# Merging a unit's last small products with the next unit's first ones, and a new order for unit 0, in a scan kernel followed by a two-layer network

## The chip, the core and the metric

The kernel runs on one core of one Trainium2 chip. The time is in microseconds (us) on the device, from launch to end. The kernel before took 334.04 us, the median of three runs (333.22 to 334.71). Engines are named as in the profile: PE (TensorE, matrix products), DVE (VectorE), ACT (ScalarE), POOL (GpSimd), SP (SyncE, which here only issues DMAs).

## What is computed

```python
# x (4, 8, 768, 32), a (4, 8, 768), B and C (4, 8, 768, 16): float32; chunk = 32
log_a = np.log(np.clip(a, 1e-06, 1.0))
for c in range(nc):                                   # chunks of the sequence
    cum = np.cumsum(la, axis=-1)
    L = np.exp(cum[:, :, :, None] - cum[:, :, None, :]) * causal
    M = np.einsum('bhin,bhjn->bhij', Cc, Bc) * L
    y_intra = np.einsum('bhij,bhjd->bhid', M, xc)
    y_inter = np.einsum('bhin,bhnd->bhid', Cc, state) * np.exp(cum)[:, :, :, None]
    y[:, :, sl] = y_intra + y_inter
    Bx = np.einsum('bhjn,bhjd->bhjnd', Bc, xc) * np.exp(cum[:, :, -1:] - cum)[:, :, :, None, None]
    state = np.exp(np.sum(la, axis=-1))[:, :, None, None] * state + np.sum(Bx, axis=2)
# y -> (3072, 256)
h = y @ w_in                                          # w_in (256, 2048)
out = (h * (1.0 / (1.0 + np.exp(-h)))) @ w_out        # w_out (2048, 256); the weights come as 64-bit floats
```

## The kernel before

**Two halves of the work.** The scan runs in units of 256 time steps: three units for each of the four batches, twelve in all, numbered 0 to 11. The network after it runs in passes of two units (512 tokens). Pass 0 is units 0 and 1, pass 1 is units 2 and 3, and so on to pass 5. While a pass of the network runs, the scan prepares the two units of the next pass.

**A unit of the scan** is made of these pieces; the letters are those of the functions and of the plan:
- loads (`L`, or `load_x`, `load_n`, `load_t`, `load_ab`, `load_pa` one by one): x, B, C and two forms of a.
- `T` (`f_T`, `f_T2`; for units 1 and 2 `f_TP` on PE): B and C are transposed, on DVE, and ACT masks the transposed C by parity of the head into `ce`.
- `P` (`f_P`, after `f_P0` clips its input): the prefix products of a, `pfx`, one scan on DVE. `C` (`f_C`): `cw` is the transposed C times `pfx`.
- `1` and `2` (`f_E1`; `f_Ab` and `f_Ek` for units 0 and 1): the decays `E` inside chunks of 64, in two scans on DVE. `B` (`f_B`): `BT`, which is B times the last decay of each chunk.
- `D`: `f_G` (line 440, the products of C and B, in tiles of 32 by 64 of the array) and `f_D0` (line 426, the products of `BT` and x, in tiles of 64 by 32), one burst on PE.
- `S`, `s` and `M`: the states between chunks (DVE), their masked copies `sm` (ACT), and the products of line 440 times `E`, written over `E` (two instructions of DVE).
- `Y`: `f_Y`, first the state products (line 480, tiles of 32 by 64), then those of the masked `E` and x (line 489, tiles of 64 by 32), one burst on PE; `f_X` copies the result to `xf` on ACT.
- `h`, `l`, `d`: `xf` is split into three parts, `xh` (ACT), `xl` and `xd` (DVE), the inputs of the network.

**PSUM.** Four of the eight banks form one tile (`bank4`) with a single buffer. The products of `D`, the result of `Y` and `B2`, a sum of the network, take it in turn. Two banks are `half` (the network's first layer, and some of the early products), two are `acc` (its output).

**A step of the network** (`step`) is a block of 128 of the 2048 hidden columns; a pass has 16 steps, f = 0 to 15. In a step PE does four products of the first layer (line 565), two of a correction for the next step (line 557), and four of the second layer for the step three earlier (lines 599 and 600); all have 512 columns. The two correction products of the second layer (line 613, `s2_d`) go into `B2`; where the four banks are in use by the scan they are put off (`PENDING`) and done together later. ACT scales (line 559), applies the activation and rounds it to `gh`. DVE makes `gl` (line 579) and `gd` (line 583); in six of the steps of passes 2 to 4 (`ASIDE`), `gl` is made by POOL. At f = 2 the outputs of the pass before are put together by DVE (lines 634 and 639), which frees `B2`.

**What sets the order.** Every engine's instructions stand in the order in which the program issues them (the schedule is manual). For passes 1 to 4 a plan says after which step each piece of the two units `a` and `b` of the next pass is issued:

```python
PLAN = {0: ("aPC",), 1: ("a1", "bL"), 3: ("aD",), 4: ("aSsM",), 5: ("aY",), 6: ("ah", "bT"), 7: ("bPC",), 8: ("b1", "aL"),
        9: ("bD",), 10: ("bSsM",), 11: ("bY",), 12: ("bh", "ald"), 13: ("bld",), 15: ("aT",)}
FIRST = {2: "a2B", 9: "b2B"}
```

`FIRST` is issued right after the large products of the first layer. The products of line 613 are put off while f is below 6 or 9 to 11. Pass 0 is written out by hand (`steps` and the text after it), since in it the weights are also brought from 64-bit to 32-bit floats: two casts on ACT (`w_size`), three instructions on DVE (`w_bits`, lines 201, 203 and 204), an addition on POOL (line 209).

**The start.** SP issues in this order: a by chunks (`ach`), C of unit 0, x of unit 0, the prefix input `pa01` of units 0 and 1 together, weights 0 to 2, then B and x of unit 1. `f_Ab` broadcasts a to the partitions by products on PE, and `f_Ek` scans from PSUM. `f_A2` (line 276) later clips a of the other batches (`acl`), which is loaded behind weight 6.

Of the kernel before, what the change touches and what calls it, by code (L numbers as in the profile page):

```python
# [33 lines left out]
def kernel(  # L34
# [49 lines left out]
    NB = 76  # L84
# [113 lines left out]
    def w_bits(n, parts=1):  # L198
        if n in raw:
            u, v, hi = two(wu.pop(n)), two(wv.pop(n)).bitcast(U32), raw[n][:, :, :, 1]  # L200
            nc.vector.tensor_scalar(out=u, in0=u, scalar1=LEAST, scalar2=MOST, op0=ALU.max, op1=ALU.min)
            u = u.bitcast(U32)
            nc.vector.tensor_scalar(out=u, in0=u, scalar1=3, scalar2=None, op0=ALU.logical_shift_left)
            nc.vector.scalar_tensor_tensor(out=v, in0=hi, scalar=0x80000000, in1=v,  # L204
                                           op0=ALU.bitwise_and, op1=ALU.bitwise_or)
            w32[n] = block("w32")
            for i in range(parts):
                fs = slice(WF // parts * i, WF // parts * (i + 1))
                nc.gpsimd.tensor_tensor(out=two(w32[n])[:, :, fs].bitcast(U32), in0=u[:, :, fs], in1=v[:, :, fs],  # L209
                                        op=ALU.add)  # L210
        if n == 3:
            load_w(n + RAW, nc.sync)
# [25 lines left out]
    pa01, pa2 = block("pa01"), block("pa2")  # L238
# [4 lines left out]
    def load_a(t, t0, n):  # L243
        nc.sync.dma_start(out=t[:, 0:n], in_=bass.AP(tensor=a.tensor, offset=a.offset + t0, ap=[[S, H], [0, N], [1, n]]))

    load_t(0, 1, nc.sync)
    load_n(0, 0, nc.scalar)
    load_x(0, nc.sync)
    load_a(pa01, 0, 2 * UT)
    for n in range(3):  # L250
        load_w(n, nc.sync)
    load_n(1, 0, nc.sync)
    load_x(1, nc.sync)

    def f_A():
        nc.vector.tensor_scalar(out=ach[A0:A1], in0=ach[A0:A1], scalar1=1.0, scalar2=1e-6, op0=ALU.min, op1=ALU.max)
        nc.vector.memset(ach[A0:A1, :, 0:1], 0.0)
        nc.sync.dma_start(out=a_first, in_=ach[A0:A1])
        load_w(3, nc.sync)
        load_w(4, nc.sync)  # L260
        load_a(pa2, 2 * UT, UT)
        load_ab(2, nc.sync)
        load_w(5, nc.sync)
        load_n(2, 1, nc.sync)
# [30 lines left out]
    def busy(n, small=0):  # L295
        t = half("zero")
        for i in range(n):
            nc.tensor.matmul(out=t, lhsT=idle[:, 0:128], rhs=idle, start=True, stop=True)
        for i in range(small):
            nc.tensor.matmul(out=t[:64, :64], lhsT=idle[:, 0:64], rhs=idle[:, 64:128], start=True, stop=True)  # L300
# [39 lines left out]
    def f_P0(u, engine):  # L340
        src = (pa2[:, 0:UT] if u == 2 else pa01[:, UT * u:UT * u + UT]).rearrange("p (c t) -> p c t", t=Q)
        PZ[u] = (pz, pz1, pz)[u]
        engine.tensor_scalar(out=PZ[u][:, :, 1:], in0=src, scalar1=1.0, scalar2=1e-6, op0=ALU.min, op1=ALU.max)
# [8 lines left out]
    def scan_E(u, g0, n, t):  # L352
        if g0 == 0:
            E[u] = sc.tile([128, 2, H, Q], FP32, name="E")
# [5 lines left out]
    def f_Ab(u, k):  # L360
        ab[u, k] = t = acc("ab").rearrange("p (h t) -> p h t", t=Q)
        n = 4 if u == 0 else H
        for h in range(0, H, n):
            nc.tensor.matmul(out=t[:, h:h + n].rearrange("p h t -> p (h t)"),  # L364
                             lhsT=sel[:A1, 2 * u + k].rearrange("r c m -> r (c m)"),
                             rhs=ach[:A1, h:h + n].rearrange("r h t -> r (h t)"), start=True, stop=True,
                             skip_group_check=True)

    def f_Ek(u, k, hs=slice(0, H)):
        t = ab[u, k] if hs.stop < H else ab.pop((u, k))  # L370
        scan_E(u, H * k + hs.start, hs.stop - hs.start, t[:, hs])
# [46 lines left out]
    def f_D0(u, ts=(0, 1, 2, 3)):  # L418
# [4 lines left out]
        for t in ts[:3 if last else 4]:  # L423
            k, c = divmod(t, 2)
            for g in range(4):
                nc.tensor.matmul(out=d[c][32 * g:32 * g + 32, k],  # L426
                                 lhsT=bt[64 * c:64 * c + 64, k, 32 * g:32 * g + 32],
                                 rhs=xc[64 * c:64 * c + 64, k, 64 * g:64 * g + 64], start=True, stop=True,
                                 tile_position=(64 * c, 32 * g), skip_group_check=True)
        BX[u] = d  # L430
        if 3 in ts:
            BT.pop(u)
# [37 lines left out]
    def f_Y(u):  # L470
        first = u % UPB == 0
        sp, cw, m, xc = SM.pop(u), CW.pop(u), E.pop(u), xt.pop(u)
        DP.pop(u)
        BX.pop(u)
        y = GY[u] = bank4()
        for t in range(1 if first else 0, 4):
            k, c = divmod(t, 2)
            for g in range(4):
# [3 lines left out]
                                 start=(k == 0 or (first and t == 2)), stop=False,  # L482
                                 tile_position=(32 * g, 64 * q), skip_group_check=True)
        for k in range(2):
            for w in range(2):
                for c in range(2):
                    for q in range(4):
# [4 lines left out]
                                         skip_group_check=True)  # L492

# [171 lines left out]
    f_P0(1, nc.gpsimd)  # L665
    load_n(1, 1, nc.gpsimd)
    f_Ab(0, 0)
    f_Ab(0, 1)
    f_TP(0)
    f_Ek(0, 0, slice(0, 4))  # L670
    f_Ek(0, 0, slice(4, 8))
    f_T(0, 1)
    for e in range(2):
        f_T2(0, e)
    f_Ek(0, 1, slice(0, 4))
    f_Ek(0, 1, slice(4, 8))
    f_B(0)
    busy(1, 10)
    f_G(0)
    f_D0(0)  # L680
    f_P(0)
    f_C(0, nc.gpsimd)
    f_A0()
    f_M(0, 0)
# [3 lines left out]
    w_size(0)  # L688
# [9 lines left out]
    w_bits(1, 2)  # L698
    f_s1(0, 0)
# [36 lines left out]
    def stage(u, what):  # L736
        for c in what:
# [6 lines left out]
            elif c == "T":  # L744
                if 0 < u < UPB:
                    f_TP(u)
                else:
                    f_T(u, 0)
                    f_T(u, 1)
                f_T2(u, 0)  # L750
# [19 lines left out]
            elif c == "Y":  # L770
                f_Y(u)
                f_X(u)
            elif c == "h":
# [9 lines left out]
    def todo(text):  # L783

        for step in text.split():
            if ":" in step:
# [6 lines left out]
    steps = ((1, 0, ""), (0, 3, "2:PTC1 s6"), (1, 1, "b5 2:2Ba"), (1, 2, "3:x b6 r11 s7"), (1, 3, ""),  # L793
             (0, 4, "2:DSsM r12"), (1, 4, "b7 r13 s8"), (0, 5, "3:T s9"), (1, 5, "2:Y b8 r14"), (0, 6, "3:1PC s10"),
             (1, 6, "b9 r15 3:2B s11 h0 l0"), (0, 7, "2:h s12"), (1, 7, "3:D b10 3:SsM"))
# [3 lines left out]
    for text in ("m0 b11 s13 2:l h1 l1", "m1 3:Y b12 s14 2:d d0 4:L 3:h h2 l2", "m2 b13 s15 3:l d1 h3 l3",  # L799
# [7 lines left out]
    PLAN = {0: ("aPC",), 1: ("a1", "bL"), 3: ("aD",), 4: ("aSsM",), 5: ("aY",), 6: ("ah", "bT"), 7: ("bPC",), 8: ("b1", "aL"),  # L807
            9: ("bD",), 10: ("bSsM",), 11: ("bY",), 12: ("bh", "ald"), 13: ("bld",), 15: ("aT",)}
    FIRST = {2: "a2B", 9: "b2B"}

    ASIDE = (2, 4, 5, 6, 10, 15)
    PENDING = []

    PARTS = {3: 10, 5: 11, 7: 12, 8: 6, 10: 13, 11: 7, 12: 14, 13: 15}

    def step(s):
# [12 lines left out]
        if scans and f in FIRST:  # L829
            stage(2 * P + 2 + "ab".index(FIRST[f][0]), FIRST[f][1:])  # L830
# [24 lines left out]
        if PENDING and not (scans and (f < 6 or 9 <= f < 12)):  # L855
            s2_d(PENDING)
            PENDING.clear()
        if scans and f == 8:
            f_sum2(P)
        if 1 <= s <= last:  # L860
            s1_gl(s - 1, nc.gpsimd if f in ASIDE and scans and P > 1 else nc.vector)
# [5 lines left out]
        if scans:  # L867
            for what in PLAN.get(f, ()):
                u = 2 * P + 2 + "ab".index(what[0])
                if f == 15 or what == "aL":  # L870
                    u += 2
                if u < NU:
                    stage(u, what[1:])
# [39 lines left out]
```

## Time and profile before

| what | value |
|---|---|
| median of three runs | 334.04 us (333.22 to 334.71) |
| the profiled execution | 334.14 us |
| its span, first to last instruction | 332.4 us, 7727 instructions |
| PE, DVE, ACT, POOL busy | 96%, 76%, 66%, 23% of the span |
| granted clock of PE | 0.996 of full speed |
| DMA | 30.80 MB, mean 93 GB/s |
| small products: lines 440, 426, 480, 489 | 8.3, 5.3, 7.9, 10.3 us busy |
| gd (line 583), gl on DVE and on POOL (line 579) | 59.6, 42.8 and 29.4 us busy |

Busy times come from one profiled execution on the chip. Products on PE are pipelined: one of 512 columns is listed with 0.39 us, but the next one starts 0.227 us after it, so costs on PE are read from the starts. The same holds on DVE, where the start of the next instruction comes a little before the listed end of the last one. `x32` behind a line of the timeline means that so many records in a row are merged into it; a small 32-bit product leaves two records, and a few records can be missing. A figure in brackets is the idle time of the engine before the instruction and what ended it.

### The profile page before, as it was taken

The numbers are of one execution on the slowest core, as the hardware profiler recorded it, in microseconds if no ns is written. First come the engines' busy times: TensorE is split into PE (matmuls) and PEld (weight loads), VectorE is DVE, ScalarE is ACT, GpSimd is POOL, SyncE is SP. The second block draws the span as 40 slices with busy tenths as digits, with TensorE's granted clock in tenths as the row PEclk, the third lists the DMA queues.
The fourth block names the chain that finished last, engine by engine and source line by source line (L and its number), as shares of the span: only waits on it lengthen the run. The fifth ranks groups of instructions, "written<-read, shape, count | busy, mean of one in ns | idle before, by whom it ended". The sixth has DMA issues, their size and how long they took to land.

```text
span 332.4 us, 7727 instructions
## 1 busy us (share of the span) xinstructions
PE 319.0 (96%) x3123; PEld 254.9 (77%) x3123; DVE 253.8 (76%) x417; ACT 218.2 (66%) x417; POOL 77.6 (23%) x77
## 2 busy tenths in 40 slices
PE   7679999999999999999999999999999999999992
PEld 4467788888878788778788778788778788888881
DVE  6794999998786987996866996866996764674453
ACT  3557488656488898667757667767657756666651
POOL 3744335465011121240202240202240202000000
PEclk9999999999999999999999999999999999999998
DMA  6999679676672863354600353600452000021003
GB/s 134 223 272 269 187 182 300 135 122 103 143 115 57 155 108 63 65 105 86 129 4 0 68 108 82 126 4 0 91 92 44 2 2 0 0 45 21 0 0 63
DMA packets 92683, 30.80 MB, mean 93 GB/s; under 512 B 77564, under 2 KB 83708, under 8 KB 92648
## 3 DMA queue, kind: packets, MB, share of 16 engines
q1 hardware_dynamic: 83848, 25.20, 34.3%
q0 software_dynamic: 2528, 4.59, 7.9%
q10 hardware_dynamic: 6272, 0.52, 1.3%
q8 instruction: 24, 0.39, 0.5%
q14 instruction: 11, 0.09, 0.1%
HBM read 22.79 MB, written 3.32 MB: 79 GB/s over the span
## 4 chain that ended last, share of the span: by engine, by line
PE 90%; DVE 3%; issue 2%; DMA 2%; SPq 1%; ACT 1%; POOL 1%; DVEq 0%; POOLq 0%; ACTq 0%
PE hp L565 23%; PE b L613 11%; PE hp L557 11%; PE oa L599 11%; PE oa L600 11%; PE oa L542 8%; PE hp L529 8%; PE gy L489 3%; PE gy L480 2%; PE gy L440 2%; DMA pa<-in_a_dram 2%; PE gy L426 1%; POOL w L209 1%; SPq L135 0%; DVE wv L204 0%
## 5 line engine op out<-in xcount | busy, mean ns | idle before, releaser
L559 ACT ACTIVATE hp<-hp 128x512 f32<-128x512 f32 x80 | 46.6, 582 | 68.1 <-PE hp L557 68.0
L579 DVE TENSOR_TENSOR gl<-g,gh 128x512 fp32r<-128x512 f32 x62 | 42.8, 690 | 50.2 <-ACT gh L575 47.2
L565 PE MATMUL hp<-xh,wh 128*128 128x512 f32 x160 | 65.3, 408 | 0.0
L583 DVE SCALAR_TENSOR_TENSOR gd<-gh,g 128x512 fp32r<-128x512 f32 x80 | 59.6, 748 | 5.1 <-ACT gh L575 5.1
L565 PE MATMUL hp<-xl,wl 128*128 128x512 f32 x160 | 62.5, 391 | 0.0
L599 PE MATMUL oa<-gh,wh 128*128 128x512 f32 x160 | 62.4, 390 | 0.0
L600 PE MATMUL oa<-gl,wl 128*128 128x512 f32 x160 | 62.3, 390 | 0.0
L579 POOL TENSOR_TENSOR gl<-g,gh 128x512 fp32r<-128x512 f32 x18 | 29.4, 1631 | 121.7 <-ACT gh L575 121.7
L575 ACT ACTIVATE gh<-g 128x512 fp32r<-128x512 f32 x80 | 50.6, 632 | 2.7
L557 PE MATMUL hp<-xd,wd 128*128 128x512 f32 x160 | 49.5, 391 | 0.0
L573 ACT ACTIVATE g<-hp 128x512 f32<-128x512 f32 x80 | 47.5, 594 | 0.5 <-PE hp L565 0.5
L613 PE MATMUL b<-gd,wd 128*128 128x512 f32 x160 | 44.3, 390 | 0.0
L565 PEld LDWEIGHTS hp<-xh,wh 128*128 128x128 f32 x160 | 30.0, 187 | 9.2 <-ACT hp L559 2.6
L557 PEld LDWEIGHTS hp<-xd,wd 128*128 128x128 f32 x160 | 30.0, 188 | 6.5
L599 PEld LDWEIGHTS oa<-gh,wh 128*128 128x128 f32 x160 | 30.0, 188 | 6.4
L613 PEld LDWEIGHTS b<-gd,wd 128*128 128x128 f32 x160 | 29.9, 188 | 6.5 <-DVE o L639 0.3
L600 PEld LDWEIGHTS oa<-gl,wl 128*128 128x128 f32 x160 | 30.0, 188 | 6.3
L565 PEld LDWEIGHTS hp<-xl,wl 128*128 128x128 f32 x160 | 30.1, 188 | 5.2
L529 PE MATMUL hp<-xf,w 128*128 128x256 f32 x128 | 29.8, 386 | 3.0 <-POOL w L209 1.7
L355 DVE TENSOR_TENSOR_SCAN E<-ab,diag 128x512 f32<-128x512 f32 (+1 forms) x26 | 29.2, 1153 | 2.0 <-PE ab L364 1.5
L209 POOL TENSOR_TENSOR w<-wu,wv 128x512 uint32<-128x512 uint32 (+1 forms) x20 | 24.1, 1212 | 27.2 <-DVE wv L204 27.1
L529 PEld LDWEIGHTS hp<-xf,w 128*128 128x128 f32 x128 | 23.7, 190 | 8.0 <-POOL w L209 2.8
(87 smaller groups left out, 384.7 us busy)
## 6 DMA issues: line engine op xcount, KB each, us to landing
ab<-a_zero SPq DMA_DIRECT2D x18, 256.0 KB
raw<-in_moe_w_in_dram SPq DMA_DIRECT2D x8, 512.0 KB
raw<-in_moe_w_out_dram SPq DMA_DIRECT2D x8, 512.0 KB
wl<-w POOLq DMA_DIRECT2D x16, 256.0 KB, 3.8
xt<-in_x_dram SPq DMA_DIRECT2D x22, 128.0 KB
out_dram<-ot SPq DMA_DIRECT2D x44, 64.0 KB
bn<-in_B_dram SPq DMA_DIRECT2D x20, 64.0 KB
tbc<-in_C_dram SPq DMA_DIRECT2D x20, 64.0 KB
```

What stands on the lines that cost most here:

```text
L355: nc.vector.tensor_tensor_scan(out=E[u].rearrange("p k h t -> p (k h t)")[:, Q * g0:Q * (g0 + n)], data0=t.rearrange("p g t -> p (g t)"), ...
L529: nc.tensor.matmul(out=hp[:, i], lhsT=two(w32[j])[:, kc, 128 * i:128 * i + 128], rhs=two(XF[u])[:, kc], start=(kc == 0), stop=(kc == KC - 1))
L557: nc.tensor.matmul(out=HP[s], lhsT=two(WD[f // 2])[:, kc, 128 * (f % 2):128 * (f % 2) + 128], rhs=XD[P][:, kc], start=(kc == 0), stop=Fals ...
L559: nc.scalar.activation(HP[s], HP[s], AF.Copy, scale=-HALF / UP)
L565: nc.tensor.matmul(out=HP[s], lhsT=two(w[f // 2])[:, kc, 128 * (f % 2):128 * (f % 2) + 128], rhs=x_[P][:, kc], start=False, stop=(kc == KC ...
L573: nc.scalar.activation(G[s], HP.pop(s), AF.Silu, scale=UP)
L575: nc.scalar.activation(GH[s], G[s], AF.Copy, scale=DOWN)
L579: engine.tensor_tensor(out=GL[s], in0=G[s], in1=GH[s].bitcast(FP32), op=ALU.subtract)
L583: nc.vector.scalar_tensor_tensor(out=GD[s], in0=GH[s].bitcast(FP32), scalar=1.0 + 1.0 / HALF, in1=G.pop(s), op0=ALU.mult, op1=ALU.subtract)
L599: nc.tensor.matmul(out=OA[P][m], lhsT=two(WH[n])[:, r, ms], rhs=gh, start=(f == 0), stop=False)
L600: nc.tensor.matmul(out=OA[P][m], lhsT=two(WL[n])[:, r, ms], rhs=gl, start=False, stop=(f == NF - 1))
L613: nc.tensor.matmul(out=B2[P][:, m], lhsT=two(WD[n])[:, r, 128 * m:128 * m + 128], rhs=gd, start=(fresh and s == tiles[0]), stop=True, skip ...
```

## The change

Three things are changed together.

**The merged burst.** `f_Y` is cut into `f_Ys` (state products) and `f_Ym` (the rest). A new function `f_YG(u)`, letter `Z`, issues for a unit and the one before it: the products of `f_G(u)`, a drain of PE, the state products of unit u - 1, `f_D0(u)`, the rest of unit u - 1's `Y`. The result of unit u - 1 goes into columns 384 to 511 of the same four banks that hold unit u's products. `E` gets a second buffer, and the pool of 2 KB blocks has 74 instead of 76.

**The plan.** Passes 1, 2 and 3 to 4 have plans of their own, in which seven pairs of units are merged (2/3, 4/5, 6/7, 7/8, 8/9, 9/10, 10/11). The pieces of the units move by up to four steps, the products of line 613 are put off to other steps (`OWN`, `LEAVE`), and POOL makes `gl` in other steps (`ASIDE`), 18 times as before. `A` and `B` are the units of the pass after next; `<` marks what is issued right after the first layer's products.

**Unit 0.** The prefix input is loaded unit by unit, unit 0's ahead of x and unit 1's behind weight 1. The broadcast products of unit 0 go to separate banks, `f_G` comes ahead of the last scan, the first `f_M` ahead of the prefix scan, and the two casts of weight 0 ahead of `f_SM`. POOL takes `cw` first, then C's load of unit 1 and the clip of unit 1; the zero columns (`f_A0`) are written later. The three instructions of `w_bits` on weight 0 are done in two halves.

```diff
-    NB = 76
+    NB = 74
...
     load_t(0, 1, nc.sync)
     load_n(0, 0, nc.scalar)
+    load_a(0)
     load_x(0, nc.sync)
-    load_a(pa01, 0, 2 * UT)
-    for n in range(3):
+    for n in range(2):
         load_w(n, nc.sync)
+    load_a(1)
+    load_w(2, nc.sync)
...
+    def f_YG(u):
+        GY[u - 1] = new_dp(u)[:, :, 384:512]
+        f_G(u)
+        nc.tensor.drain()
+        f_Ys(u - 1)
+        f_D0(u, False)
+        f_Ym(u - 1)
...
     f_P0(0, nc.gpsimd)
-    f_P0(1, nc.gpsimd)
-    load_n(1, 1, nc.gpsimd)
-    f_Ab(0, 0)
-    f_Ab(0, 1)
+    f_Ab(0, 0, slice(0, 4))
+    f_Ab(0, 0, slice(4, 8))
+    f_Ab(0, 1, slice(0, 4), half)
     f_TP(0)
     f_Ek(0, 0, slice(0, 4))
-    f_Ek(0, 0, slice(4, 8))
     f_T(0, 1)
     for e in range(2):
         f_T2(0, e)
+    f_Ab(0, 1, slice(4, 8))
+    f_Ek(0, 0, slice(4, 8))
     f_Ek(0, 1, slice(0, 4))
+    busy(1, 10, new_dp(0)[:, 0])
+    f_G(0)
     f_Ek(0, 1, slice(4, 8))
     f_B(0)
-    busy(1, 10)
-    f_G(0)
     f_D0(0)
+    f_M(0, 0)
+    w_size(0)
     f_P(0)
     f_C(0, nc.gpsimd)
-    f_A0()
-    f_M(0, 0)
+    load_n(1, 1, nc.gpsimd)
+    f_P0(1, nc.gpsimd)
     f_S(0)
     f_SM(0)
     f_M(0, 1)
-    w_size(0)
     w_bits(0, 2)
...
     w_bits(1, 2)
+    f_A0()
...
-    steps = ((1, 0, ""), (0, 3, "2:PTC1 s6"), (1, 1, "b5 2:2Ba"), (1, 2, "3:x b6 r11 s7"), (1, 3, ""),
-             (0, 4, "2:DSsM r12"), (1, 4, "b7 r13 s8"), (0, 5, "3:T s9"), (1, 5, "2:Y b8 r14"), (0, 6, "3:1PC s10"),
-             (1, 6, "b9 r15 3:2B s11 h0 l0"), (0, 7, "2:h s12"), (1, 7, "3:D b10 3:SsM"))
+    steps = ((1, 0, ""), (0, 3, "2:PTtC1 s6"), (1, 1, "b5 2:2Ba"), (1, 2, "3:x b6 r11 s7"), (1, 3, ""),
+             (0, 4, "2:DSsM r12"), (1, 4, "b7 r13 s8"), (0, 5, "3:T s9"), (1, 5, "b8 r14"), (0, 6, "3:t1P s10"),
+             (1, 6, "b9 r15 3:2B s11 h0 l0"), (0, 7, "3:Z s12"), (1, 7, "b10 3:CSsM"))
...
-    ASIDE = (2, 4, 5, 6, 10, 15)
+    PLAN1 = {0: ("atP1",), 1: ("a2B",), 2: ("aC", "bL"), 3: ("aD",), 4: ("aSsM", "bT"), 5: ("bP1",), 6: ("bt2B",),
+             7: ("bZ",), 8: ("bSM", "AL"), 9: ("bsC", "ah"), 10: ("ald",), 11: ("bY",), 12: ("bh",), 13: ("bld",),
+             15: ("AT",)}
+    PLAN2 = {0: ("atP1",), 1: ("a2B",), 2: ("aC", "bL"), 3: ("aD",), 4: ("aSM", "bT"), 5: ("as", "bP1"), 6: ("bt2B",),
+             7: ("bZ",), 8: ("bSM", "AL"), 9: ("bsC", "ah", "AT"), 10: ("ald", "AtP"), 11: ("A12",),
+             12: ("<AB", "AZ"), 13: ("bh", "ASM"), 14: ("<bld", "As", "BL"), 15: ("AC", "BT")}
+    PLAN3 = {0: ("btP1",), 1: ("b2B",), 3: ("bZ",), 4: ("bSM",), 5: ("bsC", "AL"), 6: ("ah",), 7: ("ald", "AT"),
+             8: ("AtP1",), 9: ("A2B",), 11: ("AZ",), 12: ("bh", "ASM"), 13: ("<bld", "AsC", "BL"), 15: ("BT",)}
+    OWN = {1: (9, 10, 13, 14, 15), 2: (10, 11, 15), 3: (6, 7, 8, 9, 10, 14, 15)}
+    LEAVE = {1: 10, 2: 11, 3: 10}
+    ASIDE = {1: (), 2: (4, 6, 8, 11, 13, 15), 3: (0, 4, 8, 9, 12, 15)}
```

`t` is the masking part of the old `T` (`f_T2`). With `OWN` the products of line 613 are done only in the named steps of a pass that has a scan beside it, and `LEAVE` is the step after which their sum is copied out of the banks.

## The prediction

> **What bounds the kernel now.** I read the page first: engine totals, the 40 slices, the chain that ended last.
>
> ```profile
> PE 319.0 (96%) x3123; PEld 254.9 (77%) x3123; DVE 253.8 (76%) x417; ACT 218.2 (66%) x417; POOL 77.6 (23%) x77
> PE   7679999999999999999999999999999999999992
> DVE  6794999998786987996866996866996764674453
> DMA  6999679676672863354600353600452000021003
> PE 90%; DVE 3%; issue 2%; DMA 2%; SPq 1%; ACT 1%; POOL 1%; DVEq 0%; POOLq 0%; ACTq 0%
> ```
>
> TensorE (PE) is full from the fourth slice on, and the chain is 90% PE. By stretches PE is busy in all but 0.1 us from 40 to 320 us. So every nanosecond that PE saves after 34.1 us is a gain, and every wait put into its queue there is a loss. Before 34.1 us DMA is full and VectorE (DVE) nearly so. I therefore looked at PE around two bursts of small products, in its timeline (start, us busy): a Y burst, then a G and D0 burst.
>
> ```profile
> 97.09 0.39 PE L600 MATMUL oa<-gl,wl 128*128 128x512 f32 x1
> 97.41 0.69 PE L480 MATMUL gy<-cw,sm 32*64 32x64 f32 x32
> 98.04 0.86 PE L489 MATMUL gy<-E,xt 64*32 64x64 f32 x64
> 98.83 0.50 PE L565 MATMUL hp<-xh,wh 128*128 128x512 f32 x1
> 99.16 0.39 PE L565 MATMUL hp<-xl,wl 128*128 128x512 f32 x1
> ...
> 110.53 0.39 PE L600 MATMUL oa<-gl,wl 128*128 128x512 f32 x1
> 110.85 0.69 PE L440 MATMUL gy<-ce,bh 32*64 32x128 f32 x32
> 111.47 0.43 PE L426 MATMUL gy<-xt,BT 64*32 64x64 f32 x24
> 111.83 0.50 PE L565 MATMUL hp<-xh,wh 128*128 128x512 f32 x1
> 112.17 0.40 PE L565 MATMUL hp<-xl,wl 128*128 128x512 f32 x1
> ```
>
> Large products start every 0.227 us (99.16, 99.39, 99.62 in the same timeline). Entering a burst takes 0.32 (97.09 to 97.41), 0.09 too much. Leaving it costs about 0.25: 0.15 from the last small start to the large one, and 0.11 because the next large start comes after 0.33 and not 0.227. Inside, the tile shape changes once: the last L440 start to the first L426 start is 0.198, L480 to L489 0.147, against 0.01 to 0.02 between equals.
>
> **Part 1: the merged burst.** Seven pairs are merged: units 2/3, 4/5, 6/7, 7/8, 8/9, 9/10, 10/11. A Y and a G/D0 burst carry overheads of 0.09 + 0.147 + 0.25 and 0.09 + 0.198 + 0.25, together 1.03 us. The new order is G, drain, state products, D0, rest of Y: one entry 0.09, the drain x, one shape change 0.147, one exit 0.25, so 0.49 + x. The number of products is the same. No drain of PE is in the trace. Nearest row for x: the change from L440 to L426, 0.198, where the array also empties; upper end: 0.45, that plus 0.25 for a queue that starts anew. I take 0.3, near the row. Saving 0.24 per pair, 0.1 to 0.34; for seven 1.7 us (0.6 to 2.4).
>
> A rule speaks against sharing banks. TensorEngine Tiling (Array Packing), Gotcha 1, says that different row tiles cannot access one PSUM bank simultaneously. Here L480 already sends row groups 0 and 1 to the same bank, and its 32 records start within 0.63 us, 20 ns apart, so the row shows no taking of turns. By the rule I would price the shared part at one 0.22 us product after another, some 3.5 us per pair (an estimate), and the change would lose over 20 us.
>
> **Part 2: what the merged burst waits for.** D0 needs BT, the last DVE product of the new unit (L383), and now stands in PE's queue ahead of all later large products; a late BT holds everything. Before, the second unit of a pass had six steps between D0 of the first and its own; now it has four (step 3 to step 7), shorter ones, because L613 (0.45 per step) is put off. So I walk DVE, by start-to-start times: gl and gd 0.60 each (113.41, 114.01), S 1.1, M 1.2 (94.98 to 96.18), transposes 1.03, wd 0.60, prefix scan 0.8, half an E scan 1.17 (two in 2.33), BT 0.4, two output transposes 1.22, cw 0.35.
>
> Pass 1 (units 4/5): DVE starts at 92.62 after D0 of unit 4. Three gl/gd pairs 3.66, S 1.14, M 1.2, transposes 1.03, wd 0.6, prefix 0.8, E 2.34, BT 0.4: 11.2, ready at 103.8. PE: step 4 from 92.60 to 95.01, three steps of ten large products at 0.227 to 101.82, entry 0.09, G 0.43, drain 0.3, state products 0.48, change 0.147: D0 at 103.27. Wait 0.5 (0 to 1.0).
>
> Pass 2 (units 6/7): the output sums come first and end at 141.0. The rows of DVE, and those of GpSimd (POOL) beside them:
>
> ```profile
> 139.81 1.27 DVE L639 SCALAR_TENSOR_TENSOR o<-b,o 128x512 f32<-128x512 f32 x2
> 142.21 2.38 DVE L583 SCALAR_TENSOR_TENSOR gd<-gh,g 128x512 fp32r<-128x512 f32 x2
> 148.67 1.15 DVE L583 SCALAR_TENSOR_TENSOR gd<-gh,g 128x512 fp32r<-128x512 f32 x1
> ...
> 142.07 1.36 POOL L579 TENSOR_TENSOR gl<-g,gh 128x512 fp32r<-128x512 f32 x1 [3.66 <-ACT gh L575]
> 147.99 1.29 POOL L579 TENSOR_TENSOR gl<-g,gh 128x512 fp32r<-128x512 f32 x1 [1.01 <-ACT gh L575]
> ```
>
> From 141.0: three gl/gd pairs 3.66, cw 0.35, two single gd 1.2, S 1.07, M 1.2, transposes 1.05, output transposes 1.22, prefix 0.8, E 2.34, BT 0.4: 13.3, ready at 154.3. PE: step 5 starts at 144.56, three steps to 151.37, D0 as above 1.45 later at 152.82. Wait 1.5. But two gl run on POOL in the stretch, and the rows show what that does: two gd take 2.38 instead of 1.2 beside one, one takes 1.15 instead of 0.69 beside another; a third, at 145.68, cost 0.07. Mean of 1.18, 0.46, 0.07: 0.57. Two of them add 1.15 (0.1 to 2.4). I take a wait of 2.65 (1.5 to 3.9).
>
> SBUF — State Buffer, in "SBUF: two separate sides", has the pair of ports that DVE and GpSimd share as a lock for the whole instruction. The two gd agree with it (lost 1.18 beside 1.36), the third case does not. By the rule two full gl would be lost, 1.36 + 1.29, and the wait would be 4.15 (an estimate).
>
> Units 2/3, ahead of the passes: DVE is free at 46.75 after unit 3's transposes and a weight step. One E scan 1.82 (47.35 to 49.17), prefix 0.71, weight step 1.40, E 1.25, BT 1.24 (52.87 to 54.11): 53.2. PE reaches 45.8, then three groups of eight at 0.2155, 50.9, plus 1.45: 52.4. Wait 0.8 (0 to 0.9; 0 if POOL does not slow E and BT).
>
> For 7/8, 8/9, 9/10 and 10/11 BT is ready: it ends one step or more ahead, or ahead of the output sums on which G waits already (PE idle under 0.1 at 141.14). No wait there.
>
> **Part 3: unit 0.** Its first Y burst starts at 13.81 after PE idled 2.55 on POOL's cw, which stands behind the prefix input (landed by 9.6) and two DMA issues (10.97 to 13.04). The new order takes cw ahead of these issues, puts M into DVE's idle 1.24 ahead of the prefix scan, and loads a half-sized prefix input before x. On DVE the first scan waits for one product instead of two (about 4.7, was 5.46); four scans at 0.6, a transpose 0.5, BT 0.4 end at 8.0, M (0.6, after G) at 8.9, prefix 9.6, S 10.7. On ACT sm (0.6) now stands behind weight 0's two casts (1.2), and the weight lands at about 10; so Y starts at about 11.9, 1.9 earlier (an estimate). What is late next:
>
> ```profile
> 32.46 0.42 DVE L276 TENSOR_SCALAR acl<-acl 36x512 f32<-36x512 f32 x1 [2.92 <-DMA acl<-in_a_dram]
> 33.62 0.42 DVE L410 TENSOR_TENSOR cw<-tp,pfx 128x256 f32<-128x256 f32 x1
> ...
> 34.10 5.45 PE L529 MATMUL hp<-xf,w 128*128 128x256 f32 x24 [0.54 <-DVE cw L410]
> ```
>
> DVE waits 2.92 for acl, whose DMA is queued behind the weights; DMA's share is 1.11 from 18 to 32 us. PE waits at 34.10 for unit 2's cw, which follows acl. Neither order moves acl, so PE still resumes at about 34.1 and only idles longer ahead of it. Worth 0, between -1.9 (acl lands earlier by as much) and +0.4: the zero-column DMAs of POOL (13.66 to 15.08, beside a DMA share of 0.63 to 1.01) move into the full stretch.
>
> Edits at nothing: three more DVE instructions for weight 0 and the finer first products lie ahead of the acl wait; uncovered they cost 0.3. Put-off L613 products are as many as before; their bank is free in time (M of unit 7 at about 159, the first L613 at about 162). POOL keeps 18 gl. The loads of unit 8 now land one step ahead of their transposes, but SP is not held by the steps; if they did land late, all of DVE would wait behind the transposes. The second E tile and two blocks fewer: no wait on a block is in the trace.
>
> **Sum.** -1.7 + 0.8 + 0.5 + 2.65 + 0 = +2.25. The profiled execution took 334.14 (span 332.4); that is 0.10 over the median of 334.04. 334.04 + 2.25 = 336.3 us.
>
> **The rivals.** (1) BT in time, not slower: DVE reaches BT of unit 7 before 152.8 and that of units 3 and 5 before 52.4 and 103.3. For it: DVE idles 0.95 and 1.59 between 150.8 and 155.9, so its queue is not always full. Against: those idle stretches lie behind the six steps that are now four. It gives -1.7, 332.3; it decides when the three waits sum to less than 1.7. (2) The start carries through: acl lands 1.9 earlier. For it: DMA has a gap at 16 to 17 us (share 0.63). Against: 1.11 afterwards. It gives 336.3 - 1.9 = 334.4. (3) The merge does not save what it says: x at 0.53 eats both ends. For it: no row shows a drain. With the same waits +3.95, 338.0.
>
> **How the numbers follow.** About 0.5% (1.67 us) is what a measurement of this kernel can tell from no change. The forecast 0.50, of which 0.06 lies within 0.5% (waits at their low ends: 0 + 0.2 + 1.5 - 1.7); rival 1 0.18, of which 0.03 is within 0.5%; rival 2 0.18, within; rival 3 0.14, slower. Faster 0.15, same 0.27, slower 0.58. Range: below, rival 1 at 332.3; above, all waits at their high ends (0.9 + 1.0 + 3.9) with a saving of 1.7 make 338.2, and with rival 3 a little over; I take 338.6. The forecast's own range is 335.0 to 338.2.
>
> **What would show it.** Right: PE idle of 2 to 4 us in front of D0 of unit 7 with BT as its releaser, smaller ones in front of units 3 and 5; PE's wait for unit 2's cw grown from 0.54 to some 2.4, ending at about 34; merged bursts 0.2 to 0.3 shorter than two. Wrong: no idle after 34.1, or a first continuous PE stretch that starts clearly before 33.

## The result, and the profile after

The changed kernel took 343.2 us (median of four runs, 342.46 to 344.0); the kernel before took 333.81 beside it (median of four). The ratio is 1.028 (95% interval 1.024 to 1.032). Slower was right, but the size was not: I had forecast 336.3 with a range up to 338.6. In all that follows, executions over 1.5% above the fastest of the same kernel are left out of medians and ratios. The profiled execution took 343.85 (span 342.1), 9.7 more than that of before.

The page of the changed kernel: the totals, two rows of the 40 slices, and the chain that ended last.

```profile
PE 322.9 (94%) x3122; PEld 257.2 (75%) x3123; DVE 253.3 (74%) x420; ACT 217.2 (63%) x417; POOL 77.9 (23%) x77
...
PE   8878998999999999995999999899999999999993
...
PEclk9998999999999999998999999999999999999999
...
PE 72%; DVE 14%; DMA 4%; ACT 3%; issue 3%; SPq 2%; POOL 1%; DVEq 0%; POOLq 0%; ACTq 0%
```

The chain shows most: PE carried 90% before and carries 72% now. DVE, and DMA behind it, took the difference. The PE row has a new gap in slice 19 (the wait for BT of unit 7). The clock has an 8 in slices 4 and 19; before, it was all nines until the end:

```profile
PEclk9999999999999999999999999999999999999998
```

I made a ledger by comparing the starts of the same products in both traces (first-layer products of pass 0, then each step of the passes), and of each burst with those it replaces:

| place | predicted | measured |
|---|---|---|
| unit 0 and the start, until 37 us | 0 | +0.7 |
| units 2/3 (waited 0.96 for BT) | +0.6 | +1.1 |
| pass 1, with units 4/5 (no BT wait) | +0.3 | +1.4 |
| units 6/7 (waited 3.60 for BT), and the slow products behind | +2.4 | +5.1 |
| the other four merged bursts | -1.0 | -0.6 |
| pass 3, late loads of unit 10 | 0 | +1.6 |
| rest, several small waits | 0 | +0.5 |

The first row is one draw of several. In the eleven traces that have the new unit 0 and no added products, the offset at that place lies between -1.45 and +2.47 (median -0.40).

**A merged burst without a wait**, units 7/8 in PE's timeline, answers to the two bursts of before:

```profile
178.10 0.69 PE L440 MATMUL gy<-ce,bh 32*64 32x128 f32 x32
178.95 0.69 PE L477 MATMUL gy<-cw,sm 32*64 32x64 f32 x32 [0.15 <-issue]
179.57 0.43 PE L427 MATMUL gy<-xt,BT 64*32 64x64 f32 x24
179.82 0.86 PE L491 MATMUL gy<-E,xt 64*32 64x64 f32 x64
180.61 0.50 PE L582 MATMUL hp<-xh,wh 128*128 128x512 f32 x1
```

The drain shows as 0.15 of "issue" idle. From the last start of line 440 to the first of line 477 it is 0.42 in six of the seven bursts (0.55 in that of units 4/5); I had taken 0.3. The step from line 477 to 427 costs 0.147, as predicted. The records still start some 20 ns apart although two units share the banks, so the price taken from the row held, and the one worked out from the rule on banks did not.

**The wait for BT**, PE's timeline at unit 7, and behind it two windows (length, busy time of PE, PEld, DVE, ACT, POOL, granted clock, DMA share, GB/s):

```profile
155.75 0.58 PE L477 MATMUL gy<-cw,sm 32*64 32x64 f32 x24 [0.15 <-issue]
159.93 0.58 PE L427 MATMUL gy<-xt,BT 64*32 64x64 f32 x32 [3.60 <-DVE BT L384]
```

```profile
160.00:163.50 3.50, 3.50 (x101) 2.94 (x102) 2.83 (x8) 0.66 (x2) 0.00 (x0) 0.52 0.34 85
163.50:167.00 3.50, 3.50 (x16) 2.61 (x15) 2.28 (x4) 2.34 (x5) 0.00 (x0) 0.99 0.56 86
```

The predicted wait is there, larger. What I had no term for is the clock: for 3.41 us after the wait PE runs at half of it, and large products start every 0.427 instead of 0.227. From the last large product ahead of the burst to the twentieth behind it PE takes 12.52. In gl_off (below), where the wait is 1.39 shorter and no half clock follows, it takes 9.76. So the clock costs 1.4 more.

**Why BT was late**, DVE's timeline in pass 2, three instructions that take 0.60 alone, from start to start:

```profile
145.80 1.79 DVE L596 TENSOR_TENSOR gl<-g,gh 128x512 fp32r<-128x512 f32 x1
...
152.00 1.17 DVE L596 TENSOR_TENSOR gl<-g,gh 128x512 fp32r<-128x512 f32 x1
...
156.60 1.68 DVE L600 SCALAR_TENSOR_TENSOR gd<-gh,g 128x512 fp32r<-128x512 f32 x1
```

POOL makes gl at 145.51 (1.53), 151.31 (1.31) and 156.13 (1.60). By start-to-start times DVE loses 1.11, 0.49 and 1.01, in all 2.6. DVE runs two steps behind PE here, so a third gl fell ahead of BT; I had counted two.

**The start**, PE's timeline in unit 1's Y burst:

```profile
24.52 0.43 PE L491 MATMUL gy<-E,xt 64*32 64x64 f32 x27
25.95 0.63 PE L491 MATMUL gy<-E,xt 64*32 64x64 f32 x37 [1.00 <-issue]
27.05 5.37 PE L546 MATMUL hp<-xf,w 128*128 128x256 f32 x16 [0.47 <-ACT xf L516]
```

Unit 0's Y starts at 12.25 (predicted 11.9), and PE is 1.30 ahead until 24 us. Then it waits 1.00 for nothing that the profile names, and from 27.0 to 30.4 the clock is half: the lead of 1.30 has become a lag of 1.55. (Of the wait for unit 2's cw, 0.54 before, nothing is left, since PE is late by more.)

**Pass 3**, timeline of all engines, shows a chain of four:

```profile
217.09 0.68 DVE L389 STREAM_TRANSPOSE bh<-tbc 128x256 f32<-128x256 f32 x1 [3.61 <-DMA tbc<-in_B_dram]
...
219.87 0.91 ACT L407 ACTIVATE ce<-ct,par 128x256 f32<-128x256 f32 x2 [2.14 <-DVE ct L389]
...
221.31 0.50 PE L582 MATMUL hp<-xh,wh 128*128 128x512 f32 x1 [1.35 <-ACT hp L576]
```

SP issues eight output stores from 208.34 (4.13 long), and the loads of unit 10 behind them from 212.51. DVE waits in its queue for the loads, ACT's mask waits for DVE, ACT's scaling waits behind the mask, and PE waits for that.

### The profile page after: what moved, and what is told of

Its sections match the earlier page's. It is cut to its first block, busy times and chain, and to the rows that moved or that the text cites. A ratio compares the mean times of both kernels' runs of the same rounds, so it can differ in the third digit from the quotient of the medians.

```text
span 342.1 us, 7749 instructions
## 1 busy us (share of the span) xinstructions
PE 322.9 (94%) x3122; PEld 257.2 (75%) x3123; DVE 253.3 (74%) x420; ACT 217.2 (63%) x417; POOL 77.9 (23%) x77
## 4 chain that ended last, share of the span: by engine, by line
PE 72%; DVE 14%; DMA 4%; ACT 3%; issue 3%; SPq 2%; POOL 1%; DVEq 0%; POOLq 0%; ACTq 0%
PE hp L582 19%; PE b L630 9%; PE hp L574 9%; PE oa L559 8%; PE oa L616 8%; PE oa L617 8%; PE hp L546 5%; PE gy L491 2%; DVE gd L600 2%; DVE gl L596 2%; DVE E L360 2%; DMA raw<-in_moe_w_in_dram 2%; PE gy L477 1%; DMA wl<-w 1%; DMA tbc<-in_C_dram 1%
## 5 line engine op out<-in xcount | busy, mean ns | idle before, releaser
L596 DVE TENSOR_TENSOR gl<-g,gh 128x512 fp32r<-128x512 f32 x62 | 45.1, 728 | 36.5 <-ACT gh L592 34.8
L582 PE MATMUL hp<-xh,wh 128*128 128x512 f32 x160 | 66.1, 413 | 1.6 <-ACT hp L576 1.6
L600 DVE SCALAR_TENSOR_TENSOR gd<-gh,g 128x512 fp32r<-128x512 f32 x80 | 60.5, 764 | 9.0 <-ACT gh L592 6.8
L582 PE MATMUL hp<-xl,wl 128*128 128x512 f32 x160 | 63.2, 395 | 0.1
L630 PE MATMUL b<-gd,wd 128*128 128x512 f32 x160 | 43.4, 390 | 0.0
L582 PEld LDWEIGHTS hp<-xl,wl 128*128 128x128 f32 x160 | 30.4, 190 | 5.5 <-DMA wl<-w 0.6
L546 PE MATMUL hp<-xf,w 128*128 128x256 f32 x128 | 31.1, 400 | 2.6 <-POOL w L212 1.7
L212 POOL TENSOR_TENSOR w<-wu,wv 128x512 uint32<-128x512 uint32 (+1 forms) x20 | 25.2, 1268 | 27.2 <-DVE wv L210 27.1
L546 PEld LDWEIGHTS hp<-xf,w 128*128 128x128 f32 x128 | 24.9, 199 | 7.8 <-POOL w L212 3.1
```

What stands on the lines that cost most here:

```text
L546: nc.tensor.matmul(out=hp[:, i], lhsT=two(w32[j])[:, kc, 128 * i:128 * i + 128], rhs=two(XF[u])[:, kc], start=(kc == 0), stop=(kc == KC - 1))
L582: nc.tensor.matmul(out=HP[s], lhsT=two(w[f // 2])[:, kc, 128 * (f % 2):128 * (f % 2) + 128], rhs=x_[P][:, kc], start=False, stop=(kc == KC ...
L596: engine.tensor_tensor(out=GL[s], in0=G[s], in1=GH[s].bitcast(FP32), op=ALU.subtract)
L600: nc.vector.scalar_tensor_tensor(out=GD[s], in0=GH[s].bitcast(FP32), scalar=1.0 + 1.0 / HALF, in1=G.pop(s), op0=ALU.mult, op1=ALU.subtract)
L630: nc.tensor.matmul(out=B2[P][:, m], lhsT=two(WD[n])[:, r, 128 * m:128 * m + 128], rhs=gd, start=(fresh and s == tiles[0]), stop=True, skip ...
```

## The experiments

The kernel before took 333.8 to 335.8 beside the different runs, so each ratio is against the runs beside it. Beside fill67, al_early, old_start and new_start it took 335.75, with a granted clock down to 0.981. These four ratios therefore come out low, by some 0.5% (new_start has 0.994 there and 0.999 in its second measurement), and the readings rest on the traces. Offsets are those of a step's first product against the trace of before.

**The clock behind the wait (fill67).**

```diff
         GY[u - 1] = new_dp(u)[:, :, 384:512]
+        if u == 7:
+            busy(12, 0, new_dp(u)[:, 0])
         f_G(u)
```

> The changed kernel with 12 products on constants (0.227 each, 2.7 us) in front of the merged burst of units 6 and 7, inside its wait of 3.6. Theory A, that a wait of over 3.4 costs twice, because PE then runs 3.41 us at half clock: the wait shrinks to about 0.9, D0 still starts at BT's end, no half clock after it, so 1.4 to 1.7 less than the changed kernel, about 341.7. Theory B, that the slow products after the wait come from the queue or the operands and not from the idle time: no change, 343.2, half clock as before. If the products delay anything on the path themselves: slower than 343.2.

341.81 us, ratio 1.018 (1.013 to 1.023).

```profile
159.08 0.46 PE L427 MATMUL gy<-xt,BT 64*32 64x64 f32 x32 [0.95 <-DVE BT L384]
```

The wait is 0.95, and the trace has no half clock before the end of the work. The stretch of 12.52 is 11.31 here: twelve useless products inside the wait made it 1.2 shorter, so the slow products come with the idle time. All six traces in which unit 7 waits 3.55 to 3.60 (changed kernel, al_early, own12, p01_old, old_start, after_shift) have a half clock there.

**POOL beside DVE (gl_off).**

```diff
-    ASIDE = {1: (), 2: (4, 6, 8, 11, 13, 15), 3: (0, 4, 8, 9, 12, 15)}
+    ASIDE = {1: (), 2: (11, 13, 15), 3: (0, 4, 8, 9, 12, 15)}
```

> The changed kernel with the three gl that POOL makes in steps 4, 6 and 8 of pass 2 made by DVE. Beside them three DVE instructions took 1.71, 1.09 and 1.61 instead of 0.60 each, 2.6 lost; the two gl that now stand ahead of BT of unit 7 cost DVE 1.2. Theory A, that DVE and POOL hold each other up: BT comes 1.4 earlier, PE's wait in front of D0 of unit 7 falls from 3.6 to about 2.2, and 1.4 less time, more where the half clock behind the wait goes too (341.8 to 340.3). Theory B, that the long instructions have another cause and POOL's work is a relief: BT comes 1.2 later, a wait of 4.8.

339.93 us, ratio 1.018 (1.014 to 1.021). PE's timeline:

```profile
156.48 0.46 PE L427 MATMUL gy<-xt,BT 64*32 64x64 f32 x32 [2.21 <-DVE BT L384]
```

2.2 was expected. All DVE instructions in the stretch take their usual 0.60, and here no half clock follows.

**Loads behind the stores (al_early).**

```diff
-    PLAN3 = {0: ("btP1",), 1: ("b2B",), 3: ("bZ",), 4: ("bSM",), 5: ("bsC", "AL"), 6: ("ah",), 7: ("ald", "AT"),
+    PLAN3 = {0: ("btP1",), 1: ("b2B",), 3: ("bZ",), 4: ("bSM",), 5: ("<AL", "bsC"), 6: ("ah",), 7: ("ald", "AT"),
```

> The changed kernel with the loads of the unit after next (A, the loads of units 10 and 12's place in passes 3 and 4) issued one half step earlier, ahead of the eight output stores that SP issues in step 5 of pass 3. Theory A, that SP's queue made these loads late (issued at 212.5 behind the stores, DVE waited 3.61 + 1.40 + 2.59 for them, ACT and then PE 1.35 behind DVE): the transposes find their data, PE's wait of 1.35 at 220 and the 0.1 behind it vanish, 341.7. Theory B, that the loads wait for their buffers and not for the stores: DVE waits as long, 343.2.

341.72 us, ratio 1.018 (1.012 to 1.024). The transposes at 212.68 and 213.18 wait for nothing, and PE's wait in pass 3 is gone: across that pass the offset grows by 0.06 instead of 1.65. The loads had waited for SP's queue.

**Pass 1's ACT (own12).**

```diff
-    OWN = {1: (9, 10, 13, 14, 15), ...
+    OWN = {1: (9, 10, 12, 13, 14, 15), ...
```

> The changed kernel with two of the put-off correction products of pass 1 done in step 12 instead of 13. Theory A, that in steps 12 to 14 of pass 1 ACT has 3.2 us of work a step (scale, activation, rounding, two weight casts, a copy) beside PE steps of 2.27, so that PE waits for L576 (0.21, 0.11, 0.30, 0.11 at 123.8 to 128.5): PE's steps become longer where ACT is full, these four waits mostly vanish, 0.5 to 0.7 less, 342.6. Theory B, that ACT's backlog is there anyway and only moves: the sum of the excess from 119 to 130 stays at 0.7, 343.2.

344.96 us, ratio 1.032 (1.029 to 1.035). The excess from 119 to 134 us stays (1.32 against 1.19): the four waits go, and one of 0.63 comes in front of line 582, for a weight whose cast on ACT was late. The backlog only moves; theory A fell.

**The first four units in the old order (p01_old).**

```diff
-    PLAN1 = {0: ("atP1",), 1: ("a2B",), 2: ("aC", "bL"), 3: ("aD",), 4: ("aSsM", "bT"), 5: ("bP1",), 6: ("bt2B",), 7: ("bZ",), ...
+    PLAN1 = {0: ("atPC",), 1: ("a1", "bL"), 2: ("<a2B",), 3: ("aD",), 4: ("aSsM",), 5: ("aY",), 6: ("ah", "bTt"),
+             7: ("bPC",), 8: ("b1", "AL"), 9: ("<b2B", "bD"), 10: ("bSsM",), 11: ("bY",), ...
```

The order of pass 0 and, in pass 1, the steps of the products of line 613 are those of before as well.

> The changed kernel with the first four units in the old order: units 2/3 and 4/5 not merged, pass 1 by the old plan; passes 2 to 4 and the start are the changed kernel's. Theory A, by the ledger of the two traces (2/3: 1.14 lost; pass 1: 1.46 lost to ACT's late scaling and casts, 0.05 to the burst): the offset against the kernel before at the start of pass 2 falls from 3.25 to about 0.7 (less where no half clock falls into the start), and the time by 2.5, to about 340.6. Theory B, that the old plan of pass 1 leaves pass 2 with later loads or a fuller ACT: the loss comes back in pass 2, less than 1 us gained.

340.75 us, ratio 1.014 (1.010 to 1.018). The offset is +0.01 at pass 1's first step and +0.09 at pass 2's; it was 1.88 and 3.25 (0.7 of both lies in the start, which came out at 0.0 here). From there it grows to 7.37, by 7.3; in the changed kernel it grows by 6.6. So most of the loss arises behind pass 1.

**Unit 0 by itself (new_start, old_start, new_start_again).** The diff is the part on unit 0 shown above, alone in the kernel before, or alone taken out of the changed one.

> The kernel before with the new unit 0 alone (no merged burst, no new plan). Theory A, that the start is worth nothing by itself because DVE's wait for acl and unit 2's cw hold PE until 34.1: Y of unit 0 starts near 12.3 instead of 13.8, PE waits at 34 for cw of unit 2 for more than 1.5 instead of 0.54, the time stays within 0.5 of before's 333.8. Theory B, that the lead of 1.3 to 1.5 of unit 0 survives, since the trace of the changed kernel shows no wait for that cw any more: about 332.4. Theory C, that what was lost in the changed kernel before 34 us (a stretch of 3.41 at half clock from 27.0, 1.00 without a named releaser at 24.96) belongs to the new order itself: the same loss here, about 334.5.

> The changed kernel with unit 0's old order. By the offsets of the two traces the start lost 0.7 of the 9.4, so theory A (the rest is the merged bursts and the plan): 342.5, with BT waits in front of D0 of units 3 and 7 as large as in the changed kernel (1.0 and 3.6). Theory B, that unit 0's order also moved the weights' DMA and with it the later waits: below 341, smaller waits at units 3 and 7.

> The new unit 0 alone, as in the first call, beside it on the same chip: 0.994 of the kernel before if that was no accident of the chip; 1.000 if the kernel before falls into half clock in its start less often here. Its granted clock should again be 0.996 or more in most executions.

new_start: 334.2 us, ratio 0.994 (0.991 to 0.998); again: 334.28, ratio 0.999 (0.997 to 1.001). In the two traces PE's continuous stretch starts at 33.70 and 33.50 instead of 34.10, after a wait of 0.71 and 0.80 for unit 2's cw (and 1.37 and 1.05 for its B before that); the nameless wait of 1.00 and the half clock are absent. So cw did hold PE, and the lead there is 0.4 to 0.6. At the end of the work it is still 0.6 in the second trace, and in the first a lag of 0.4. What more the first ratio shows lies in the kernel before: among its thirteen executions beside new_start are 334.14 at a mean granted clock of 0.996, 335.05 at 0.991, 336.88 at 0.986 and 338.02 at 0.981, while new_start was at 0.996 or more in all ten runs. old_start: 344.65, ratio 1.026 (1.020 to 1.033); on 333.8 that is 342.6, as theory A had it, though the interval takes in the changed kernel's ratio. Its trace is that of an execution of 349.18 at a mean clock of 0.971; its waits at units 3 and 7 are 0.95 and 3.57, as theory A had them, and nothing more is read from it.

**All mends together (mended):** p01_old, al_early and gl_off in one.

> The last one together with the two edits that worked: loads ahead of the stores in pass 3, no gl on POOL in steps 4, 6 and 8 of pass 2. If the ledger adds up: 343.2 - 2.5 (first four units) - 1.5 (loads) - 1.4 and 1.5 (wait of units 6/7 and the half clock behind it) = 336.3, with a BT wait of 2.2 left at unit 7 and no half clock after the start. If the parts were not independent (DVE fuller without POOL, ACT's backlog moved into pass 2), 338 or more.

337.44 us, ratio 1.005 (1.002 to 1.007), between the two theories. In the trace the offset is -1.45 at pass 1, which is the luck of this execution's start, -1.18 at pass 2, and +2.51 at the end. From pass 1 on it loses 4.0 where the changed kernel loses 8.0. What is left is mainly the BT wait of 2.17 at unit 7 and a half clock of 3.41 behind it, which I had expected to be gone. By the starts this clock costs 1.1, so the two are 3.3 together; the rest is not accounted for.

**The merge alone (late_merge, late_merge2, late_merge2_new).**

```diff
-    PLAN = {..., 5: ("aY",), 6: ("ah", "bT"), 7: ("bPC",), ..., 9: ("bD",), 10: ("bSsM",), ...
+    PLAN = {..., 6: ("bTt",), 7: ("bPC",), ..., 9: ("<b2B", "bZ"), 10: ("bSsM", "ah"), ...     # late_merge
+    PLAN = {..., 6: ("bTt",), 7: ("bP",), ..., 9: ("<b2B", "bZ"), 10: ("bSsCM", "ah"), ...     # late_merge2
```

> The kernel before (its start, its plan, its steps for the products of line 613) with one difference: in each of the four passes the first unit's Y burst is put off from step 5 to step 9 and merged there with the second unit's G and D0, where BT is in time already. A test of the merge by itself. By the measured bursts (merged 2.70 without a wait; apart 1.61 + 1.18, 1.55 + 1.21, 1.61 + 1.21, 1.73 + 1.18): 0.05 to 0.2 less for each, 0.4 to 0.5 in all, ratio 0.999. My prediction's 0.24 for each would be 1.0, ratio 0.997. Theory B, that ACT's copy, masks and rounding now meet in steps 9 and 10 and PE waits for line 576: slower by 0.5, ratio 1.0015.

> The same late merge, with the new unit 0. Its gains should add: the new start alone ran at 0.994 of the kernel before, the late merge at 0.999 by the row above, together 0.993. If the gain of the start is only that PE falls into half clock less often at the beginning, the trace shows no half clock before the end, and the least time is about that of the kernel before's least.

late_merge took 361.89, late_merge_new (the same with the new start) 362.41. I had overlooked that cw has one buffer: DVE waited 7.73 to write the second unit's cw until the merged burst had read the first one's, and BT stood behind it:

```profile
111.42 0.43 DVE L410 TENSOR_TENSOR cw<-ct,pfx 128x256 f32<-128x256 f32 x1 [7.73 <-PE gy L476]
```

Each of the four bursts waited 5.05 to 5.17 and was followed by 6.83 us of half clock: one wait inside a merged burst costs some 7 us.

> The late merge with one step moved: cw of the second unit is made after the merged burst (step 10) and not in step 7. Theory A, that the 5.1 of the first try was a circle (cw has one buffer, its writing waited 7.7 for the first unit's state products, which now stand in the merged burst, and BT behind cw on DVE): no BT wait, 0.4 to 0.5 less than the kernel before, ratio 0.999. Theory B, that another single tile (x's two buffers, bn) makes the same circle: a BT wait of over 3 again and over 350.

> The same with the new unit 0. New start at 0.994 and late merge at 0.999: ratio 0.993, about 332.3 where the kernel before takes 334.6; least time near 331.3.

Without the circle they took 342.06 (ratio 1.017, 1.013 to 1.021) and 340.81 (1.017, 1.012 to 1.021). BT is in time, yet the gain does not come. PE's timeline of late_merge2 in the burst of units 6/7:

```profile
162.45 0.87 PE L490 MATMUL gy<-E,xt 64*32 64x64 f32 x61
165.44 0.30 PE L490 MATMUL gy<-E,xt 64*32 64x64 f32 x3 [2.13 <-issue]
```

**Instructions (after_shift, late_shift, late_shift2).** The wait of 2.13 has no releaser. If all records of PE in the trace (products, weight loads, semaphore waits, drains) are counted from the start, it stands at record 3520; the others of late_merge2 stand at 704, 2496 and 4544, and the 1.00 of the changed kernel at 704: always 192 past a multiple of 256. Each ends 1.3 to 2.0 us after a 16 KB transfer on the instruction queue has landed. A merged burst issues 306 records in 2.5 us. To test it, products on constants in PE's idle time shift all that follows by 90 records:

```diff
-    busy(1, 10, new_dp(0)[:, 0])
+    busy(1, 55, new_dp(0)[:, 0])                     # after_shift, late_shift
...
     f_D0(1)
+    busy(0, 45, new_dp(1)[:, 2, 256:384])            # late_shift2
```

> The changed kernel with 45 more small products on constants in PE's idle time ahead of unit 0's Y burst: 90 more PE instructions, so that every later one stands 90 places further on. Theory A, that PE's idle times without a named releaser are waits for its next 256 instructions (in all traces so far they end at record 192 of a group of 256, 1.3 to 2.0 after an instruction transfer of 16 KB has landed, and only where 256 instructions are used up in some 3 us): the 1.00 at 25 us in unit 1's Y burst goes (records 675 to 867, only the border at 704), and a new one appears in the merged burst of units 4/5 (records 2230 to 2536, borders 2240 and 2496) of 0.5 to 2, where there was none. Theory B, that these idle times belong to the place in the schedule (DMA load, operands): 1.0 at 25 us as before, none in the burst of units 4/5.

> The late merge with the new unit 0 and the same 45 small products. It had idle times without releaser of 0.71 at 25, 0.53, 1.81 and 1.66 in or behind the merged bursts of units 4/5, 6/7 and 8/9 (borders 2240/2496, 3264/3520, 4288/4544 both in the burst or right behind it), and a half clock behind the second. Theory A (borders of 256 instructions): moved by 90, no merged burst holds two borders (only 2496; 3520; 4544; 5568), all four idle times go and the half clock with them: 340.8 - 4.7 - 1.7 = 334.4, which is what the new start takes alone, as the merge by itself is worth next to nothing. Theory B: the idle times stay where they are, 340.8.

> The late merge with the new unit 0, and the 45 small products now in PE's idle 1.33 at 20.6 us, behind unit 1's D0: the records ahead of them stay where they were, those behind move by 90. Theory A (borders of 256 instructions): no idle time without a releaser of over 0.6 in the start (unit 0's Y at 216 to 392, unit 1's at 675 to 867, one border each) and none in the merged bursts, so no half clock either, or one at most in the start; the merge is worth 0 to 0.15 for each of four: 0.2 to 0.5 under the new start alone, ratio to the kernel before 0.993. Theory B (the idle time moves to yet another burst): one of 0.5 or more in the start, about the kernel before.

after_shift (346.18, ratio 1.032): the burst of units 4/5 stops where it was said to, at record 2496:

```profile
106.23 0.67 PE L491 MATMUL gy<-E,xt 64*32 64x64 f32 x44
107.47 0.41 PE L491 MATMUL gy<-E,xt 64*32 64x64 f32 x20 [0.57 <-issue]
```

The stop in unit 1's Y burst did not go, as theory A had said. It is 0.54 long and stands at record 704 again, where another product now comes:

```profile
24.81 0.45 PE L477 MATMUL gy<-cw,sm 32*64 32x64 f32 x14
25.80 0.50 PE L477 MATMUL gy<-cw,sm 32*64 32x64 f32 x18 [0.54 <-issue]
```

So the stop belongs to the record and not to the product, but in the start one border in a burst is enough. Two more came that I had not named: 0.70 in the burst of units 2/3, which now holds two borders too, and 0.63 at record 448 in unit 0's Y, where the added products had used up the records. late_shift (335.34, ratio 1.000, 0.998 to 1.003): no such wait in any merged burst. One of 1.02 came in unit 0's Y, at border 448, with a half clock behind it, and one of 0.54 stands at border 704. late_shift2 (334.35, ratio 0.999, 0.996 to 1.002): again none in the merged bursts, and one of 1.67 at border 704 in the start, so theory B holds for the start. In these two the merge can be read by itself. In late_shift2 the offset goes from +1.81 at pass 1 to +1.49 at the end, 0.08 gained for each of four; in late_shift it goes from +1.94 to +1.95. Without a merge it stays between -0.59 and -0.65 in new_start_again, and moves from -0.39 to +0.39 in new_start. So the merge is worth 0 to 0.08 each, less than what two executions of one kernel can differ by.

## Why the prediction was wrong

The sum was +2.25, and the two traces differ by 9.7. The step that failed is part 2, the price of a merged burst that has to wait for BT, together with waits of other engines that the sum put at nothing. Of the 7.5 that the ledger has above the sum, 2.7 lie at units 6/7, 1.6 in pass 3, 1.1 in pass 1 and 0.7 in the start. The stated range was also narrower than its own terms: all waits at their high ends without a saving make 334.04 + 5.8 = 339.8, not 338.6.

**The size of the saving (part 1).** 0.24 for each pair was predicted. Measured were 0.15 for each of the changed kernel's four bursts in the ledger's fifth row, 0.08 in late_shift2 and nothing in late_shift. The drain costs 0.42 and not 0.3; with that the step gives 0.12. Rival 3 (x at 0.53) had the right mechanism at a smaller size.

**The waits (part 2), where the main step failed.** Which units would wait was right for two of three. Unit 3 waited 0.96 (0.8). Unit 5 did not: PE came to it 0.8 later than I had worked out, because of ACT and the drain. Unit 7 waited 3.60 (2.65, up to 3.9). The mis-sized term is POOL: 2.6 measured against 1.15, from a third gl that DVE's lag put into the stretch, and from a mean that took in the one case with nearly no overlap. (Without POOL's 2.6 the wait would have been 1.0, less than the 1.5 of the sum.) The three losses (1.11, 0.49, 1.01) are close to the overlaps in the timelines (1.24, 0.62, 1.13). This is what SBUF — State Buffer, "SBUF: two separate sides", says of the shared ports, and against my choice.

**What the sum had no term for.** A wait of PE was priced at its length. It also costs clock: 1.4 us behind unit 7 and 1.65 in the start; fill67 shows that it comes with the idle time. TensorE: Matmul & The Clock Gate, "HAM oscillation — how this bites in real kernels", warns of idle gaps of over 3.4 us. The wait of 3.60 agrees; but 2.17 was enough in mended, 2.05 in own12's start, 1.81 in late_merge2_new, and in the changed kernel's start 1.00 and 0.47 with small products between them, while 2.21 in gl_off was not.

**Unit 0 (part 3).** The mechanism was right: in new_start cw of unit 2 holds PE until 33.5 to 33.7. In the changed kernel's trace the lead was lost before it came to that, to the instruction wait and the clock. Rival 2 did not come about there (DVE takes acl at 32.19; before, 32.46), but in single executions it did in part: in mended acl comes at 31.01, and PE stays 1.45 ahead.

**Edits at nothing.** "SP is not held by the steps" was the wrong sentence: in pass 3 the stores of step 5 stand ahead of the loads of step 5. I named what would follow (all of DVE behind the transposes) but walked only unit 8's loads, not unit 10's: 1.6. Pass 1's put-off products and moved copies met the weight casts on ACT, an engine that I did not walk in the passes: 1.4 (0.7 to 1.5 in the other traces with this plan). That they were the cause is shown only together with the merge of units 4/5 (p01_old takes all of it back); own12 did not separate them.

What stays open: how much idle time in which place halves the clock, and whether an order of the start exists that keeps both its lead and its instruction supply.

## What to carry to other kernels

Before a burst of small products is put ahead of the main stream, walk every engine and every queue to its latest input: a wait there stops everything, and is paid again in half clock once it is long enough. Two short bursts with large products between them leave time for the clock, the instruction supply and the single buffers; one long burst tests all three. Price each merge from one pair measured alone, before a plan of seven is written around it.

## What the runs showed of the hardware

- PE's instructions come in 16 KB transfers, one for each 256 records: 24 for 6300 records in the changed kernel's trace, 25 for 6390 in after_shift. Where a merged burst used up 256 in about 3 us, PE stopped at the border for 0.5 to 2.1 us. The burst of units 6/7 in after_shift also holds two borders, but waits 3.56 for BT between them, and has no such stop. In the start (DMA share about 1) PE also stopped at a slower pace, at record 704 when the transfer landed at 24.40 (changed kernel, 1.00) and not when it landed at 22.86 (new_start). Runtime: NRT & Kernel Launch, "Instruction fetch mechanics", gives the blocks of 256 instructions and calls the cost of crossing one mostly hidden; in these bursts it is not.
- Half clock comes in stretches of 3.41 or 6.83 us. An estimate from the mean clocks listed with new_start: the kernel before had from none to about three of the short ones in its work from one execution to the next (0.005 of clock is 3.41 us at half), which goes roughly with its times of 334.1 to 339.0.
- A drain of PE between products of 32 by 64 took 0.42 from start to start, in six of the changed kernel's seven bursts and in all four of late_shift2.
